# One attention and mixing kernel, with the order of its operations on all engines written anew

## The chip, the cores and the metric

The kernel runs on one core of a Trainium2 chip. Its engines work in parallel, each through its own queue in order: TensorE (PE, matrix products), VectorE (DVE), ScalarE (ACT), GpSimd (POOL) and SyncE (SP, which here only issues DMAs). An engine waits at the head of its queue until the semaphores tell that the operands are there; whatever stands behind it waits too. The metric is the device time of the core in microseconds (us), the median of several runs.

## The reference

Two blocks follow each other. The first is attention with a polynomial sketch, for 4 batches of 4 heads, 1088 tokens and 32 values a head:

```python
def phi(x):
    a = np.einsum('rd,bhsd->bhsr', S1, x)
    b = np.einsum('rd,bhsd->bhsr', S2, x)
    return np.einsum('bhsi,bhsj->bhsij', a, b).reshape(*x.shape[:-1], r * r)
q_p, k_p = (phi(q), phi(k))
kv = np.einsum('bhsf,bhsd->bhfd', k_p, v)
z = np.sum(k_p, axis=2)
num = np.einsum('bhsf,bhfd->bhsd', q_p, kv)
den = np.einsum('bhsf,bhf->bhs', q_p, z)[..., None] + 1e-06
```

with r = 8, so 64 features. Its output num / den, with the four heads side by side, is x (4 x 1088 x 128) for the second block:

```python
theta = x @ w_theta
cos_t, sin_t = (np.cos(theta), np.sin(theta))
yr = np.einsum('ts,bsd->btd', w_tok_r, x * cos_t)
yi = np.einsum('ts,bsd->btd', w_tok_i, x * sin_t)
u = x + yr + yi
return (u + np.maximum(u @ w_ch, 0.0)).astype(np.float32)
```

The two token matrices are 1088 x 1088. They, the sketch matrices and the small weights come as 64-bit floats and are turned into 32-bit ones on the chip.

## The kernel before, in words

A recording layer (`Layout`) takes down 1005 operations. Each has an engine, a function that issues one or several instructions, and the buffers that it writes and reads; its number is its place in that record. The record is the same in both kernels. Three tables then say how it is issued. `ORDER` lists all operation numbers in one sequence; each engine's queue, the DMA queues of SP, ACT and POOL among them, is the part of this sequence that belongs to it. `SLOTS` gives each of the buffers one of the numbered pieces of its memory class (22 large pieces of 1152 words, 5 for raw weights, 8 PSUM banks and so on); an operation that takes a piece over waits for the last reader of its former content. `GAPS` puts filler products (`spin`, 128 x 384, their result is never read) ahead of nine operations, 27 in all.

The stages, with names as in the code, a batch number behind them:

- **loads**: k, q and v of each batch, 576 KB each; 17 token rows `row` of 1088 KB; `loadh`, a second copy of k for three batches.
- **grid, keys, sums, rest, chain**: the keys are split into a rounded part and a remainder, and 32 x 32 products over 9 chunks give the sum of the key features exactly enough for the denominator. `sums` and `rest` use 32 columns of the TensorE array at a time. `chain` turns these sums, in turns of TensorE, DVE and ACT, into the matrix of the level products; its operations 86 to 94 are those of batch 0. The last of them, 94 (`cut`), writes what `levels` of batch 0 needs.
- **kT, kf, kv**: three transposes, an ACT copy, the feature products, a DVE outer product, then the products with v (64 columns on 32 columns of the array).
- **qscale, qT, q0, levels, den, num**: the queries are scaled and split; `levels` gives their features against the chain's result; DVE forms the denominator; `num` is the numerator.
- **theta, mix**: the phase products, sine and cosine on ACT, and the products with the token rows. `mix0` and `mix1` (batches 0 and 1) use 17 rows over 1088 tokens. Batches 2 and 3 share seven half-size products (`m1` to `m7`, `zc` and `ac` are their differences), added up by `acc`.
- **out**: the last product, and the stores.

Each weight row costs two ACT passes and two DVE passes (`weight`, lines 576 to 582) before TensorE can use it.

The operations that the text names by number are: 8 (a small ACT pass for the sketch matrix), 20 (POOL, the block form of that matrix, needed by all `kf`), 27 (DVE, a small slice of three instructions), 52 and 53 (the grid of batch 0), 55 (DVE, the rounded keys of batch 0), 57 to 65 (`sums0`), 67 to 75 (`rest0`), 78 (ACT, the squares of q of batch 0 with their sum), 79 (TensorE, the one-column product that adds this sum over the partitions), 86 (`chain0`, first products), 87 (DVE, its mask), 89 (DVE, split), 90 (second products), 94 (cut), 98 (first `kf0`), 99 (the ACT copy behind it), 101, 107 and 113 (`kv0`), 120, 126 and 132 (`kT1`), 148 to 155 (`sums1`), 158 to 168 (`rest1`), 203 and 197 (`kT2`), 205 (`kf2`), 216 (DVE, the rounded keys of batch 2), 219 to 227 (`sums2`), 229 to 237 (`rest2`), 247 (the ACT copy of `kT3`), 248 (`kf3`), 274 to 282 (`sums3`), 284 to 292 (`rest3`), 307 (first products of `chain2`), 462, 469, 476, 562, 569, 576 (`num`).

Of the kernel before, what the change touches and what calls it, by code (L numbers as in the profile page):

```python
# [31 lines left out]
RPS = 4  # L32
EARLY = (2, 60.0, 4.0)
ORDER = (
# [43 lines left out]
)  # L78
GAPS = {11: 3, 57: 3, 79: 3, 110: 1, 203: 8, 153: 1, 77: 5, 86: 2, 163: 1}
SLOTS = (  # L80
# [11 lines left out]
)  # L92
WARM = 0
LOAD_LEAD = 60.0
RAW_LEAD = 30.0
CHAINS = ((0,), (1,), (2, 3))
QPOOL = (False,) * 4
KEEP = (2, 3)
KEEP_CLS = "big"
PAIR = (2, 3)  # L100
QUADS = (2, 3)
QTURN = (3,)
XTURN = (1, 2, 3)
# [1385 lines left out]
```

## Time and profile before

| | |
|---|---|
| median of 3 runs | 215.11 us (215.11 to 215.16) |
| profiled execution | 214.93 us, span 213.2 us |
| granted TensorE clock, mean | 0.996 |
| TensorE busy | 206.8 us |
| DVE busy | 181.0 us |
| ACT busy | 113.1 us |
| POOL busy | 40.3 us |
| read from HBM | 29.84 MB |

The span is the time from the first to the last instruction of the program; the execution has 1.7 us around it. In a row of TensorE, a line such as `PE L333 MATMUL ps<-hf 128*32 128x32 bf16 x28` says: the function at line 333 issued it, the result goes to a PSUM tile, the weights are 128 rows by 32 columns of the array, 32 columns stream through, and 28 such instructions follow each other. A 32-bit product shows as two instructions. Most products are issued by one helper at line 333, so they are told apart by their tiles: `sbk,g` are feature products, `hf` the key sums, `ident` transposes, `sm,ones` sums over the partitions, `idle` fillers, `big,zs` the mixing. The time of a TensorE row includes the tail of its last product, which overlaps the next row; the difference of two starts is what the queue was held.

### The profile page before, as it was taken

The numbers are of one execution on the slowest core, as the hardware profiler recorded it, in microseconds if no ns is written. First come the engines' busy times: TensorE is split into PE (matmuls) and PEld (weight loads), VectorE is DVE, ScalarE is ACT, GpSimd is POOL, SyncE is SP. The second block draws the span as 40 slices with busy tenths as digits, with TensorE's granted clock in tenths as the row PEclk, the third lists the DMA queues.
The fourth block names the chain that finished last, engine by engine and source line by source line (L and its number), as shares of the span: only waits on it lengthen the run. The fifth ranks groups of instructions, "written<-read, shape, count | busy, mean of one in ns | idle before, by whom it ended". The sixth has DMA issues, their size and how long they took to land.

```text
span 213.2 us, 5209 instructions
## 1 busy us (share of the span) xinstructions
PE 206.8 (97%) x2092; PEld 150.0 (70%) x2092; DVE 181.0 (85%) x363; ACT 113.1 (53%) x238; POOL 40.3 (19%) x89
## 2 busy tenths in 40 slices
PE   7999999999999999999999999999999999999991
PEld 7777798968867677756686665766667768667671
DVE  1799999999999999999998999987999986583632
ACT  3899999999999699664435203686600000000000
POOL 1272730306800106600000005000400000040001
PEclk9999999999999999999999999999999999999998
DMA  6999999996996526867300005438253010070043
GB/s 217 407 416 416 377 353 422 425 347 111 358 302 205 235 114 176 346 212 276 152 0 0 3 0 86 132 113 232 51 87 65 0 31 0 3 125 1 14 75 68
DMA packets 28779, 37.05 MB, mean 174 GB/s; under 512 B 21332, under 2 KB 23812, under 8 KB 26580
## 3 DMA queue, kind: packets, MB, share of 16 engines
q1 hardware_dynamic: 23268, 31.91, 43.2%
q0 software_dynamic: 1488, 3.15, 7.1%
q10 hardware_dynamic: 4000, 1.67, 3.0%
q8 instruction: 16, 0.26, 0.5%
q14 instruction: 7, 0.06, 0.1%
HBM read 29.84 MB, written 4.00 MB: 159 GB/s over the span
## 4 chain that ended last, share of the span: by engine, by line
PE 78%; issue 10%; ACT 5%; DMA 2%; DVE 2%; POOL 1%; POOLq 0%; SPq 0%; DVEq 0%; ACTq 0%
PE ps L333 71%; PE ps L1063 2%; DMA st<-s 2%; PE ps L961 2%; ACT big L627 2%; POOL out L1246 1%; ACT g L732 1%; PE ps L362 1%; ACT big L934 1%; PE ps L729 1%; ACT big L579 1%; ACT big L577 1%; PE ps L1136 0%; DVE big L313 0%; DVE g L1250 0%
## 5 line engine op out<-in xcount | busy, mean ns | idle before, releaser
L333 PE MATMUL ps<-big,zs 128*128 128x384 f32 (+2 forms) x380 | 109.0, 435 | 0.0
L333 PEld LDWEIGHTS ps<-big,zs 128*128 128x128 f32 x380 | 67.1, 190 | 34.3 <-issue 0.5
L1287 ACT COPY g<-ps 80x256 f32<-80x256 f32 x1 | 0.4, 367 | 55.1 <-PE ps L1280 55.1
L577 ACT ACTIVATE big<-zs 128x1088 f32<-128x1088 f32 x17 | 20.8, 1226 | 6.5 <-issue 4.0
L579 ACT ACTIVATE big<-zs 128x1088 int32<-128x1088 uint32 (+1 forms) x18 | 21.4, 1191 | 3.2 <-DVE big L313 2.2
L313 DVE CUSTOM_DVE_ANT_0 big<-big,big 128x2176 uint16<-128x2176 uint16 x17 | 21.9, 1285 | 0.0
L333 PE MATMUL ps<-big,big 128*32 128x32 f32 (+2 forms) x352 | 21.7, 234 | 0.0
L313 DVE TENSOR_TENSOR big<-big,big 128x544 f32<-128x544 f32 x24 | 16.5, 715 | 2.6 <-PE ps L333 2.5
L333 PEld LDWEIGHTS ps<-big,big 128*32 128x32 f32 (+1 forms) x352 | 14.7, 124 | 4.9 <-issue 0.8
L327 POOL DMA_DIRECT2D g<-big x6 | 5.3, 1088 | 59.9 <-ACT g L1223 59.0
L1246 POOL DMA_DIRECT2D out<-g x6 | 3.8, 633 | 51.8 <-DVE g L1250 51.8
L317 DVE TENSOR_SCALAR big<-big 128x1088 int32<-128x1088 int32 x17 | 12.1, 719 | 0.0
L333 PEld LDWEIGHTS ps<-w,big 128*128 128x128 f32 (+1 forms) x76 | 9.9, 189 | 2.2 <-ACT big L1076 0.6
L362 PE MATMUL ps<-idle 128*128 128x112 bf16 (+1 forms) x67 | 10.0, 312 | 1.3 <-POOL idle L364 1.3
L313 DVE TENSOR_TENSOR g<-lv 128x768 f32<-128x768 f32 x12 | 11.0, 949 | 0.1
L320 DVE SCALAR_TENSOR_TENSOR big<-ps,even,big 128x160 f32<-128x160 f32 (+1 forms) x10 | 5.0, 495 | 7.0 <-PE ps L333 6.6
L313 DVE TENSOR_TENSOR big<-big,hf 128x1152 f32<-128x1152 f32 x8 | 10.7, 1349 | 0.0
L333 PE MATMUL ps<-w,big 128*128 128x128 f32 (+1 forms) x76 | 10.7, 278 | 0.0
L333 PE MATMUL ps<-sbk,g 128*128 128x64 f32 x72 | 10.0, 276 | 0.3 <-ACT g L732 0.3
L333 PE MATMUL ps<-mf,big 128*128 128x96 f32 (+1 forms) x72 | 10.2, 279 | 0.0
L313 DVE TENSOR_TENSOR zs<-zs,g 128x384 f32<-128x384 f32 (+2 forms) x24 | 9.9, 448 | 0.1
L333 PEld LDWEIGHTS ps<-sbk,g 128*128 128x128 f32 x72 | 9.0, 191 | 0.8 <-ACT g L732 0.6
(200 smaller groups left out, 354.8 us busy)
## 6 DMA issues: line engine op xcount, KB each, us to landing
zs<-w_tok SPq DMA_DIRECT2D x17, 1088.0 KB, 8.5
big<-k_l SPq DMA_DIRECT2D x5, 576.0 KB, 12.4
big<-v_l SPq DMA_DIRECT2D x4, 576.0 KB, 15.5
big<-q_l SPq DMA_DIRECT2D x3, 576.0 KB, 10.4
big<-hf POOLq DMA_DIRECT2D x3, 576.0 KB, 9.9
far<-zs SPq DMA_DIRECT2D x3, 576.0 KB, 3.0
zs<-far SPq DMA_DIRECT2D x12, 144.0 KB, 2.8
big<-k_l ACTq DMA_DIRECT2D x2, 576.0 KB, 4.5
```

The costliest lines, as they stand in the source:

```text
L313: eng.tensor_tensor(out=o, in0=a, in1=b, op=f)
L317: (eng or V).tensor_scalar(out=o, in0=a, scalar1=s1, scalar2=s2, op0=op0, **kw)
L320: (eng or V).scalar_tensor_tensor(out=o, in0=a, scalar=s, in1=b, op0=op0, op1=op1)
L327: op("G", 0.9, lambda: G.dma_start(dst(), src(), accum_op=ALU.add), w, r, fly=fly)
L333: T.matmul(o, lhs, rhs, start=start, stop=stop, skip_group_check=True)
L362: T.matmul(nowhere()[:, :n], idle()[:, 0:P], idle()[:, :n], start=True, stop=True, skip_group_check=True)
L577: op("A", 0.22 + n * 0.0009, lambda: A.activation(dfn(), words_of(raw(), n)[1].bitcast(F32), AF.Prelu, scale=2.0**-112, alpha=-(2.0**32)), ...
L579: op("A", 0.22 + n * 0.0009, lambda: A.activation(stp(), words_of(raw(), n)[0].bitcast(U32), AF.Copy, scale=2.0**-29), [stp], [raw])
L627: op("A", act(n) + 0.1, lambda: A.activation(flat(r()), kc(), AF.Square, accum_out=km()[:, 1:2]), [r, (km, 1)], [kx])
L961: T.transpose(tr()[:, i * P:(i + 1) * P], x()[:, g * GC + i].rearrange("p h d -> p (h d)"), ident())
L1063: T.transpose(tr()[:, i * P:(i + 1) * P], qp()[:, i * H + 2 * n:i * H + 2 * n + 2].rearrange("p h i j -> p (h i j)"), ident())
L1246: E.dma_start(out[b, s0:s0 + n, f * SQ:(f + 1) * SQ].rearrange("(c j) i -> j c i", j=SQ), ot()[f * SQ:(f + 1) * SQ, :n].rearrange("j (c i) ...
```

## The change

`ORDER` and `SLOTS` are replaced; nothing else is. The first 25 entries of `ORDER` stay, up to operation 144: the DMAs of the first ten loads and the sketch, and the first operations on them. Behind them the sequence is new on all five engines, and the buffers' pieces with it. The operations, their shapes and the nine places of the fillers (each ahead of the same operation as before) are the same. The lines of `ORDER` up to the second chain, old and new:

```diff
 ORDER = (
-    0, 1, 29, 32, 4, 2, 5, 3, 34, 30, 358, 50, 33, 102, 44, 96, 6, 108, 103, 36, 7, 51, 368, 54, 144, 8, 97, 10, 9,
-    11, 55, 109, 20, 52, 12, 57, 139, 58, 59, 60, 61, 62, 63, 126, 13, 31, 132, 56, 98, 127, 265, 14, 393, 128, 143,
-    246, 15, 145, 64, 65, 67, 68, 78, 35, 69, 16, 70, 19, 148, 149, 150, 151, 152, 269, 99, 66, 79, 247, 53, 80, 100,
-    110, 129, 17, 133, 130, 359, 25, 363, 81, 271, 83, 18, 203, 360, 361, 71, 41, 153, 104, 272, 210, 197, 353, 258,
-    45, 146, 72, 198, 73, 204, 248, 43, 259, 84, 26, 105, 362, 241, 74, 154, 325, 249, 214, 75, 82, 27, 327, 370, 106,
-    155, 270, 28, 47, 76, 250, 111, 46, 77, 147, 388, 216, 85, 328, 86, 21, 329, 326, 87, 112, 205, 88, 330, 242, 89,
-    120, 48, 243, 90, 206, 331, 121, 252, 369, 91, 332, 92, 134, 93, 101, 378, 394, 94, 122, 140, 253, 156, 107, 123,
-    141, 371, 135, 260, 169, 142, 124, 95, 441, 438, 157, 22, 136, 364, 439, 115, 444, 217, 440, 445, 174, 442, 261,
-    372, 446, 337, 443, 158, 159, 160, 161, 345, 365, 447, 266, 244, 170, 113, 448, 171, 373, 162, 354, 172, 215, 449,
-    163, 164, 165, 166, 211, 39, 191, 167, 173, 450, 114, 168, 212, 175, 245, 451, 333, 176, 192, 177, 267, 452, 338,
-    117, 37, 453, 343, 268, 334, 116, 254, 118, 454, 344, 341, 355, 178, 335, 273, 455, 193, 366, 342, 119, 199, 179,
-    456, 125, 255, 464, 346, 389, 219, 131, 457, 137, 465, 200, 467, 180, 367, 466, 458, 181, 194, 468, 49, 460, 459,
-    182, 471, 469, 461, 336, 183, 356, 462, 470, 339, 184, 472, 463, 474, 256, 138, 478, 383, 473, 475, 42, 185, 486,
-    390, 476, 480, 398, 340, 274, 374, 220, 221, 275, 276, 251, 186, 40, 277, 222, 278, 257, 544, 481, 477, 541, 488,
-    376, 494, 23, 375, 38, 489, 479, 195, 542, 496, 188, 482, 545, 497, 483, 357, 538, 484, 487, 218, 539, 546, 485,
-    543, 377, 24, 213, 187, 189, 223, 224, 225, 226, 279, 280, 498, 540, 547, 281, 548, 190, 549, 282, 284, 285, 490,
-    286, 287, 288, 289, 379, 227, 290, 291, 292, 503, 504, 505, 550, 495, 492, 491, 493, 551, 552, 553, 228, 385, 262,
-    506, 507, 263, 499, 500, 554, 229, 230, 555, 283, 293, 380, 294, 231, 556, 304, 301, 384, 232, 196, 233, 234, 235,
-    236, 502, 295, 305, 564, 395, 399, 501, 237, 565, 296, 264, 557, 413, 238, 566, 567, 568, 403, 571, 560, 561, 239,
-    558, 559, 297, 298, 569, 574, 306, 572, 386, 381, 575, 302, 382, 240, 303, 391, 562, 387, 573, 563, 576, 570, 581,
-    582, 307, 577, 308, 309, 404, 583, 584, 586, 578, 396, 310, 392, 508, 509, 311, 585, 400, 312, 595, 313, 510, 314,
+    0, 1, 29, 32, 4, 2, 5, 3, 34, 30, 358, 50, 33, 102, 44, 96, 6, 108, 103, 36, 7, 51, 368, 54, 144, 10, 35, 52, 393,
+    31, 97, 8, 9, 55, 363, 132, 126, 53, 139, 109, 11, 265, 12, 20, 143, 57, 58, 59, 60, 61, 62, 98, 127, 13, 56, 145,
+    269, 99, 14, 100, 246, 271, 15, 16, 25, 17, 63, 64, 128, 247, 78, 65, 66, 83, 79, 67, 146, 270, 68, 129, 69, 18,
+    110, 104, 360, 70, 111, 80, 84, 148, 149, 150, 112, 151, 130, 81, 45, 210, 133, 272, 46, 248, 47, 21, 359, 105,
+    249, 26, 71, 361, 106, 72, 203, 197, 147, 204, 198, 370, 250, 73, 74, 353, 82, 205, 75, 76, 41, 120, 362, 214,
+    325, 326, 77, 329, 85, 86, 87, 27, 241, 330, 88, 152, 153, 154, 155, 258, 327, 216, 328, 388, 89, 28, 331, 252,
+    253, 242, 90, 243, 121, 48, 134, 259, 206, 369, 91, 332, 92, 93, 94, 95, 122, 101, 371, 215, 135, 136, 217, 169,
+    107, 156, 113, 123, 157, 124, 394, 260, 114, 261, 373, 365, 438, 444, 266, 140, 439, 364, 440, 372, 441, 445, 446,
+    442, 158, 170, 159, 160, 443, 447, 211, 19, 23, 341, 22, 244, 343, 212, 171, 141, 115, 24, 161, 162, 191, 163,
+    164, 448, 449, 450, 245, 342, 219, 165, 166, 43, 167, 116, 142, 273, 344, 174, 220, 335, 254, 172, 192, 255, 451,
+    168, 333, 117, 175, 176, 177, 173, 336, 267, 452, 354, 334, 453, 118, 337, 345, 338, 193, 119, 199, 274, 454, 455,
+    346, 194, 178, 456, 464, 179, 125, 275, 221, 222, 131, 137, 465, 457, 180, 389, 467, 466, 460, 461, 223, 458, 181,
+    468, 256, 339, 218, 182, 459, 469, 183, 200, 138, 470, 49, 462, 471, 472, 184, 356, 340, 463, 474, 478, 185, 186,
+    479, 473, 355, 475, 486, 276, 277, 278, 480, 481, 279, 280, 224, 188, 213, 281, 488, 489, 282, 284, 251, 357, 374,
+    376, 476, 195, 541, 477, 482, 544, 545, 494, 375, 377, 283, 225, 542, 496, 484, 497, 538, 539, 483, 485, 546, 226,
+    227, 285, 286, 540, 543, 547, 287, 288, 289, 187, 268, 40, 228, 290, 257, 495, 291, 292, 366, 498, 189, 548, 490,
+    262, 549, 503, 504, 190, 229, 500, 378, 230, 380, 550, 39, 367, 551, 293, 491, 304, 294, 295, 552, 301, 302, 42,
+    196, 231, 232, 383, 233, 553, 234, 499, 379, 487, 492, 493, 554, 502, 235, 236, 263, 237, 555, 238, 239, 264, 556,
+    390, 395, 384, 37, 38, 505, 296, 501, 506, 564, 507, 565, 385, 566, 297, 567, 568, 298, 557, 398, 560, 558, 403,
+    305, 561, 571, 559, 381, 306, 569, 240, 303, 572, 573, 574, 570, 413, 307, 575, 562, 563, 382, 576, 386, 391, 308,
...
```

The rest of `ORDER` and all of `SLOTS` change in the same manner.

67 rows, old and new, of tables (ORDER, SLOTS) are left out of this document.

## The prediction

> **What bounds the kernel now.** I read the busy times first, then the engines stretch by stretch, then TensorE's own waits.
>
> ```profile
> PE 206.8 (97%) x2092; PEld 150.0 (70%) x2092; DVE 181.0 (85%) x363; ACT 113.1 (53%) x238; POOL 40.3 (19%) x89
> ```
>
> Stretches: PE, weight loads, DVE, ACT and POOL busy, granted clock, DMA share, GB/s.
>
> ```profile
> 10.00:20.00 10.00, 9.74 (x205) 7.88 (x203) 9.61 (x20) 9.88 (x26) 4.85 (x17) 1.00 1.02 418
> 20.00:30.00 10.00, 9.99 (x198) 7.94 (x198) 9.62 (x27) 9.29 (x27) 4.72 (x12) 1.00 1.02 366
> 40.00:110.00 70.00, 70.00 (x833) 49.98 (x832) 68.30 (x127) 55.96 (x103) 16.53 (x28) 1.00 0.69 232
> 110.00:205.00 95.00, 95.00 (x530) 64.75 (x529) 77.26 (x141) 22.11 (x45) 7.85 (x10) 1.00 0.27 57
> ```
>
> TensorE's waits over the whole span:
>
> ```profile
> PE ps L362 <- POOL idle L364: 1.3, 1, 1.3
> PE ps L333 <- ACT g L732: 0.3, 1, 0.3
> PE ps L333 <- DVE hf L317: 0.2, 1, 0.2
> ```
>
> TensorE is full from 10 us to the last product, and DVE is nearly full up to 110 us (68.30 of 70.00). The set of products is the same in both kernels, the 27 filler products of the gaps too. So an order can win only waits and changeover losses inside TensorE's queue; what it adds there is paid in full, since no later stretch has idle time to give back. The end (the last six products, outputs, stores) has the same operations in nearly the same order, and I cost it at nothing.
>
> **The waits that the change can take away.** TensorE's rows (start, time, operation, count):
>
> ```profile
> 6.98 0.65 PE L362 MATMUL ps<-idle 128*128 128x384 bf16 x3
> 7.70 0.27 PE L416 MATMUL ps<-ident,m 128*2 128x128 f32 x1
> 7.81 0.65 PE L362 MATMUL ps<-idle 128*128 128x384 bf16 x3
> 8.68 0.35 PE L333 MATMUL ps<-hf 128*32 128x32 bf16 x28 [0.23 <-DVE hf L317]
> ...
> 11.84 0.22 PE L333 MATMUL ps<-hf 128*32 128x32 bf16 x8
> ...
> 12.70 0.66 PE L362 MATMUL ps<-idle 128*128 128x384 bf16 x3
> 13.20 0.28 PE L333 MATMUL ps<-sm,ones 128*128 128x1 f32 x2
> ...
> 18.34 0.25 PE L333 MATMUL ps<-big,big 128*32 128x32 f32 x8
> 18.41 0.25 PE L333 MATMUL ps<-big 128*32 128x32 f32 x8
> 18.92 0.88 PE L333 MATMUL ps<-sbk,g 128*128 128x64 f32 x6 [0.26 <-ACT g L732]
> ...
> 23.58 0.25 PE L333 MATMUL ps<-sq,sm 32*32 32x16 f32 x8
> ...
> 25.59 0.83 PE L333 MATMUL ps<-sm,pbd 128*128 128x64 f32 x6
> ...
> 27.80 0.54 PE L333 MATMUL ps<-g,big 128*32 128x64 f32 x24
> ```
>
> A filler holds the queue 0.16 us (from 12.70 to 13.20 three of them pass; their 0.65 includes the last one's tail). Three from 6.98 end their issue at 7.47, the next product starts at 7.70: 0.23 lost. Three from 7.81 end at 8.30, the key sums start at 8.68: 0.38, of which 0.09 is a changeover, below. The feature product at 18.92 stands 0.44 behind the last eight strips (eight take 0.07, from 18.34 to 18.41), 0.33 of it a wait. That makes 0.23 + 0.29 + 0.33 = 0.85 us of waits. All may go: the transposes of key tile 1 (126, 132) now stand ahead of the fillers at the first two places, and the feature product 248 stands behind other work.
>
> **The waits that it adds.** I lay the new queues out by hand, each operation with its row's duration.
> First, product 79 (the query scale) needs the ACT pass 78:
>
> ```profile
> 11.74 1.15 ACT L934 ACTIVATE big<-big 128x1152 f32<-128x1152 f32 x1
> 12.80 0.19 ACT L934 ACTIVATION_READ_ACCUMULATOR big<-big 128x1 f32 x1
> 12.89 0.22 ACT L744 COPY sm<-ps 128x96 f32<-128x96 f32 x1
> ...
> 13.08 0.49 ACT L732 COPY g<-ps 128x384 f32<-128x384 f32 x1
> ```
>
> On ACT the copies 99 and 247 (0.22 and 0.49, each some 0.1 less where the next one overlaps it) move ahead of it, so it ends at about 13.5 instead of 12.98 (11.74 to 12.80 + 0.19). On TensorE most of the strip work from 11.84 to 12.70 moves behind 79, so TensorE is there at about 12.6 instead of 13.2: 0.9 us of waiting. Ahead of that, the small ACT pass 8 moves behind two copies; DVE's key rounding 55 and POOL's block 20 slide by 0.35, and the products 57 and 98 that need them wait about 0.4 together.
>
> Second, the chain of head group 0 (operations 86 to 94, TensorE, DVE and ACT in turn):
>
> ```profile
> 20.64 0.18 DVE L317 TENSOR_SCALAR psc<-ps 128x32 f32<-128x32 f32 x1
> 20.86 0.42 DVE L313 TENSOR_TENSOR psc<-ps,psc 128x32 f32<-128x32 f32 x2
> ...
> 23.22 0.87 DVE L317 TENSOR_SCALAR hf<-big,sm 128x1152 bf16<-128x1152 f32 x1
> 24.03 0.22 DVE L313 TENSOR_TENSOR sm<-ps,hm 128x64 f32<-128x64 f32 x1
> ...
> 27.83 0.16 DVE L317 TENSOR_SCALAR sm<-sm 128x4 int32<-128x4 int32 x1
> ```
>
> With the waits above, and with 205 and 120 ahead of them, the chain's first products (23.58) come at about 24.6. DVE has by then done all that stands ahead of its mask and idles some 1.3 us, from 23.8 to 25.1. Behind the mask now stand 27 (0.6, from 20.64 to 20.86 + 0.42) and 216 (0.81, from 23.22 to 24.03), so the split 89 ends at about 27.0, and TensorE, which has only short work in between, waits 0.5 us at product 90 (25.59 before, 27.1 now). The cut 94 (27.83) starts at about 29.7, with as much DVE work ahead of it as before: DVE is then 1.9 us behind. The level products come after further feature products and don't wait.
>
> Added: 0.4 + 0.9 + 0.5 = 1.8; taken away 0.85; net **+0.95 us**. Bounds: -0.85, if every new wait is covered, and +1.9, if TensorE later loses all that DVE has lost.
>
> **Changeovers.** Products on strips of the array (32 or 64 columns wide) and on the whole array:
>
> ```profile
> 33.95 0.49 PE L961 MATMUL ps<-ident,big 128*128 128x128 f32 x3
> 34.37 0.46 PE L333 MATMUL ps<-big,big 128*32 128x32 f32 x32
> 34.76 0.55 PE L961 MATMUL ps<-ident,big 128*128 128x128 f32 x3
> ...
> 39.61 0.82 PE L961 MATMUL ps<-ident,big 128*128 128x128 f32 x6
> 40.27 0.78 PE L333 MATMUL ps<-sbk,g 128*128 128x64 f32 x6
> ```
>
> Six transposes followed by whole-array work hold the queue 0.66, so three 0.33; three followed by strips hold it 0.42: 0.09 to go into strips. 32 strip products at 0.07 for eight take 0.28; they hold it 0.39: 0.11 to come out. So 0.2 for each run of strips. Counted over the queue, the old order has 34 runs and the new one 38. Up to the level products of batch 0 they are equal; behind them 14 become 18 (158 | 159, 160 | 161, 162 alone where 158 to 161 were one, 223 alone, 225 alone, 291 and 292 alone, 235 apart from 229; in exchange 113 goes in front and 307 joins 562). Four runs, all where TensorE has no idle time: **+0.8 us**; bounds 0 (they fall into waits) and 1.2.
>
> One rule speaks against this term. The Trainium skill, "TensorE: Matmul & The Clock Gate", section "Step-by-step: what each phase is for", has TensorE pull the next weights ahead of products in flight when the row groups don't conflict or the background weight buffer takes them. By it a changeover is hidden, and the sum would be the waits alone. Between whole-array products the rows agree (0.11 a transpose, without a gap); between strips and the whole array they show the 0.2.
>
> **What costs nothing.** The loads: the first ten are in place; behind them q1 goes ahead of v0, h3 and h2 come earlier, v1 and v3 later. The DMA engines are full at least to 30 us either way (share 1.02), with the same bytes.
>
> ```profile
> big<-v_l SPq DMA_DIRECT2D x4, 576.0 KB, 15.5
> ...
> 12.35 0.33 SPq L605 DMA_DIRECT2D big<-q_l x1
> ```
>
> v0 takes q1's place, issued at 12.35, and lands by 27.9 with the median; its first product stood at 27.80 and now comes near 29.5. That cover is thin, 1.6 us; if it fails, the value sums wait and the level products of batch 0 behind them. POOL's joins keep their places or come earlier. From 110 us on, DVE and ACT have room (77.26 and 22.11 of 95): a new place there costs nothing as long as each partial result is read before its bank is written again, and between product 6 and product 7 of the same bank there are now some 1.4 us of other products.
>
> **Sum.** Against the profiled execution (214.93 us, span 213.2): 214.93 + 0.95 + 0.8 = 216.7. It lies 0.18 below the median of the runs, 215.11; on that the same sum gives 216.9. I forecast **216.8 us**.
>
> **Rivals.**
> Covered (not slower): the old waits go and no new one of weight comes, because ACT gets through its early copies sooner than I laid out and 78 ends before TensorE is there. For it: these are short waits, and a few tenths on ACT decide. Against it: ACT is 9.88 of 10.00 busy there, so a pass behind 0.5 us more work does come later. 215.1 - 0.85 + 0.8 = 215.1; if the changeovers too fall where TensorE would wait, 215.1 - 0.85 = 214.3, faster. It decides where the new waits stay under 0.5 us in all (0.85 - 0.8 + 0.43). Chances 0.14 and 0.08.
> Free changeovers: only the waits count, 216.0. For it the rule above, against it the rows. 0.10.
> DVE becomes the bound: the 1.9 us it loses by 29.7 stay, since it idles only 1.7 from 40 to 110, and TensorE waits for it at the rotated level products and the second chains: 215.1 + 1.9 + 0.8 = 217.8. For it DVE's share, against it that TensorE itself comes 1 to 1.8 later, which hides most. 0.20.
> A late load: if v0 takes 3.3 us more than the median to land, it is 1.7 past its cover, 218.5. 0.06.
>
> **How the numbers follow.** The forecast itself has 0.42 (own range 216.3 to 217.3). 0.2% is 0.43 us, about what a measurement tells from no change here. Faster is 0.08, same 0.14, slower 0.42 + 0.10 + 0.20 + 0.06 = 0.78. The range 215.0 to 218.0 leaves out the 0.08 below and the late loads, and takes in the DVE bound.
>
> **What would show it.** Right: a wait of 0.5 to 1 us of the one-column product on ACT's L934 at 13 us; DVE waiting about 1 us on L333 near 25; the cut's first row near 29.7; and 0.09 and 0.11 at the two ends of each strip run, as now. Wrong: no new PE wait in the first 30 us, or a PE wait beyond 40 us, which would be a DVE or load wait; a span under 213.5 would mean that the covers hold.

## The result, and the profile after

The changed kernel takes 220.15 us in the median (219.41 to 223.46, 4 executions) against 215.13 us of the kernel before, run beside it. The ratio is 1.022, with an interval of 1.020 to 1.024: slower by 5.0 us. The forecast was 216.8 us, with 215.0 to 218.0 as its range: the direction was right, and the size a third of what came. Of the changed kernel the profiled execution took 219.41 us, with a span of 217.6 us. (The intervals given with ratios leave out executions more than 1.5% above the fastest; the medians and ranges do not.)

The first thing to see is new: before, the slices of the granted clock read 9 up to the last one, which reads 8. The page of the changed kernel, busy times and granted clock:

```profile
PE 209.4 (96%) x2092; PEld 152.4 (70%) x2092; DVE 181.5 (83%) x363; ACT 113.9 (52%) x238; POOL 44.8 (21%) x89
...
PEclk9999979999999999999999999999999999999999
```

The stretches of the changed kernel (PE, weight loads, DVE, ACT, POOL busy, granted clock, DMA share, GB/s):

```profile
10.00:20.00 10.00, 9.28 (x180) 7.53 (x178) 9.83 (x19) 9.08 (x26) 5.47 (x14) 1.00 1.02 416
20.00:30.00 10.00, 9.51 (x200) 8.00 (x202) 8.43 (x21) 8.94 (x23) 6.04 (x13) 0.97 1.03 396
30.00:40.00 10.00, 10.00 (x206) 8.92 (x198) 8.16 (x16) 7.30 (x19) 8.22 (x20) 0.86 1.02 408
40.00:110.00 70.00, 69.97 (x861) 49.89 (x856) 67.17 (x130) 58.23 (x112) 13.70 (x22) 1.00 0.67 225
...
28.00:29.00 1.00, 1.00 (x12) 1.00 (x11) 1.00 (x2) 1.00 (x2) 0.00 (x0) 1.00 1.01 320
29.00:30.00 1.00, 1.00 (x36) 0.93 (x39) 0.90 (x5) 1.00 (x4) 0.00 (x0) 0.74 1.04 331
30.00:31.00 1.00, 1.00 (x52) 1.00 (x48) 0.86 (x6) 0.81 (x5) 0.25 (x1) 0.50 1.02 333
...
32.00:33.00 1.00, 1.00 (x10) 1.00 (x10) 1.00 (x2) 0.36 (x3) 0.86 (x3) 0.55 1.02 410
```

From 10 to 20 and from 20 to 30 us TensorE falls 0.72 and 0.49 short of full, where it fell 0.26 and 0.01 short before; DVE is no fuller than before from 40 to 110 (67.17 for 68.30). TensorE is counted as busy throughout from 28 to 33 us, and still it loses time there: its clock is granted at 0.50. The trace's record of clock changes has the halving at 29.48 us and the return at 32.89, 3.41 us later.

TensorE's waits in the changed kernel:

```profile
PE ps L362 <- POOL idle L364: 1.3, 1, 1.3
PE ps L333 <- DMA g<-big: 0.7, 1, 0.7
PE ps L333 <- ACT big L934: 0.5, 1, 0.5
PE ps L333 <- DVE sm L313: 0.5, 1, 0.5
PE ps L333 <- DVE hf L317: 0.2, 1, 0.2
PE ps L333 <- POOL sq L313: 0.2, 1, 0.2
PE ps L416 <- DVE m L435: 0.2, 1, 0.2
```

Two of the forecast waits are there (on ACT's L934 and on DVE's split). Two were not forecast: 0.2 us for POOL's `sq` at 17.10 us, and a wait on the DMA `g<-big`, late in the kernel. The rows behind the three longest, on TensorE:

```profile
13.23 0.38 PE L333 MATMUL ps<-sm,ones 128*128 128x1 f32 x2 [0.52 <-ACT big L934]
...
26.97 0.83 PE L333 MATMUL ps<-sm,pbd 128*128 128x64 f32 x6 [0.49 <-DVE sm L313]
...
142.96 0.81 PE L333 MATMUL ps<-g,w 128*128 128x320 f32 x2 [0.73 <-DMA g<-big]
```

and on DVE, the idle time ahead of the mask 87, and the cut 94:

```profile
23.08 0.33 DVE L317 TENSOR_SCALAR sm<-sm 128x1 int32<-128x1 int32 x2
24.73 0.22 DVE L313 TENSOR_TENSOR sm<-ps,hm 128x64 f32<-128x64 f32 x1 [1.33 <-PE ps L333]
...
29.27 0.17 DVE L317 TENSOR_SCALAR sm<-sm 128x4 int32<-128x4 int32 x1
```

Where the time comes from is read from the starts of four operations that stand in the same order in both kernels: 90 (second products of the first chain), 442 (last level product of batch 0), 752 (first numerator product of batch 3) and 1003 (the last store). The starts in us, the last columns being the differences:

```
                     90      442      752     1003   442-752   752-1003
before             25.59    33.20   133.20   209.60   100.00    76.40
after              26.97    35.98   137.13   214.09   101.15    76.96
```

The changed kernel is 1.4 us late at 90, 2.8 us at 442, loses 1.15 more up to 752 and 0.56 behind it. So there are four places: the first 27 us, the half clock between 90 and 442, the middle, and the end. The experiments take them one by one.

One thing must be kept in mind with this table. The four operations stand in the same order, but some others have changed sides. The products 113 and 266 come ahead of 442 in the new order and behind it in the old one, where they hold the queue 0.36 and 0.14 us. So of the 2.78 us at 442, 0.50 is work done earlier, and the middle loses 0.50 more than the table says: 1.65 for the same work. In the same way 0.33 of the 1.38 at 90 are the three transposes 252 (`kT3`), which the old order has behind it. The eight products that change sides at 752 nearly cancel (2.58 us each way in the old kernel).

### The profile page after: what moved, and what is told of

Read it like the earlier page. It is cut to its first block, busy times and chain, and to the rows that moved or that the text cites. A ratio compares the mean times of both kernels' runs of the same rounds, so it can differ in the third digit from the quotient of the medians.

```text
span 217.6 us, 5203 instructions
## 1 busy us (share of the span) xinstructions
PE 209.4 (96%) x2092; PEld 152.4 (70%) x2092; DVE 181.5 (83%) x363; ACT 113.9 (52%) x238; POOL 44.8 (21%) x89
## 4 chain that ended last, share of the span: by engine, by line
PE 67%; issue 14%; DVE 9%; DMA 5%; POOL 2%; ACT 1%; POOLq 0%; SPq 0%; DVEq 0%; ACTq 0%
PE ps L333 60%; DVE big L313 3%; DMA g<-big 3%; PE ps L1063 2%; DMA st<-s 2%; PE ps L961 2%; DVE hf L317 1%; PE ps L362 1%; POOL out L1246 1%; PE ps L729 1%; POOL sx L536 1%; DVE zs L313 1%; PE ps L1136 1%; DVE sm L317 0%; DVE g L1250 0%
## 5 line engine op out<-in xcount | busy, mean ns | idle before, releaser
L333 PE MATMUL ps<-big,big 128*32 128x32 f32 (+2 forms) x352 | 23.4, 235 | 0.0
L333 PEld LDWEIGHTS ps<-big,big 128*32 128x32 f32 (+1 forms) x352 | 15.3, 125 | 6.3 <-issue 0.9
L333 PE MATMUL ps<-mf,big 128*128 128x96 f32 (+1 forms) x72 | 10.7, 282 | 0.0
L333 PE MATMUL ps<-sbk,g 128*128 128x64 f32 x72 | 10.6, 288 | 0.1
L333 PEld LDWEIGHTS ps<-sbk,g 128*128 128x128 f32 x72 | 9.6, 203 | 0.5 <-POOL sbk L313 0.2
L333 PEld LDWEIGHTS <-hf 128*32 128x32 bf16 (+1 forms) x252 | 7.9, 98 | 2.7 <-issue 0.9
```

The source lines that it names most:

```text
L333: T.matmul(o, lhs, rhs, start=start, stop=stop, skip_group_check=True)
```

## The experiments

### The clock

First, two ways to fill the thin places of the new order with fillers: eight more, or the same 27 moved.

```diff
 # e1_fill, the changed kernel
-GAPS = {11: 3, 57: 3, 79: 3, 110: 1, 203: 8, 153: 1, 77: 5, 86: 2, 163: 1}
+GAPS = {11: 3, 57: 3, 79: 3, 110: 1, 203: 8, 153: 1, 77: 5, 86: 2, 163: 1, 90: 4, 122: 2, 101: 2}
 # e1_move, the changed kernel
+GAPS = {11: 3, 57: 3, 79: 3, 110: 1, 203: 8, 153: 1, 77: 1, 86: 0, 163: 1, 90: 4, 122: 2}
```

> The changed kernel with eight fillers more: four ahead of product 90 (in its 0.5 us wait), two ahead of 122 and two ahead of 101. Theory 1 (the granted clock at half from 29.5 to 32.9 us costs some 1.5 us, in some executions more often, and comes from too little streaming in the array in the 3.4 us before): the clock stays at 1.00 from 6 to 210 us, the median falls by 1 to 1.5 us to about 218.8 and the executions agree within 0.5 us. Rival (the clock dip costs nothing, since TensorE waits for DVE there anyway): the median rises by the fillers outside the wait, 0.8 us, to about 221.

> The changed kernel with six of the seven fillers ahead of 77 and 86 put ahead of 90 (four) and 122 (two); 27 in all, as before. Theory 1 plus the chain as bound: the first products of chain 0 come 0.9 us earlier, DVE idles 1 us less ahead of its mask, and the clock stays up: about 217.5. If the clock alone counts: 218. Rival (DVE's lateness does not reach TensorE, the dip does not cost): 220, as the changed kernel.

e1_fill: 220.02 us (219.71 to 220.32). The clock is whole and the spread falls from 4 us to 0.6, but the median stays, between the two expected values. The eight fillers hold the queue 1.3 us, of which the wait at 90 hides some; at 442 the profiled execution is 0.5 ahead of the changed kernel's. It loses more than that again in the middle (102.27 us for 101.15), most of it in two pauses at 43 and 49 us for which its profile shows no operand that was waited for. What makes them is open. e1_move: 218.52 us (three executions at 218.08 to 218.60, one at 222.32), 1.6 less than the changed kernel with as many fillers. Its profiled execution has the full clock and reaches 442 at 34.46, which is 1.26 behind the old kernel instead of 2.78. The half clock thus made about 1.5 us in the profiled execution of the changed kernel. A second execution of the changed kernel (e8_again, below), which has its half clock elsewhere, says the same: from 90 to 442 it takes 7.57 us instead of 9.01, which is 1.4.

I call what halves the granted clock the gate. Does it belong to the new order? The old kernel without fillers, and without seven of them:

```diff
 # g1_nofill, the kernel before
-GAPS = {11: 3, 57: 3, 79: 3, 110: 1, 203: 8, 153: 1, 77: 5, 86: 2, 163: 1}
+GAPS = {}
 # b3_gate, the kernel before
+GAPS = {11: 3, 57: 3, 79: 3, 110: 1, 203: 8, 153: 1, 163: 1}
```

> The kernel before without any of its 27 filler products. If the clock gate closes after stretches in which TensorE streams little, whatever the order, the old order too must lose its full clock somewhere in the first 30 us, by 1.3 to 1.7 us for each stretch of 3.4 us at half speed: 217 to 220 us, differing from execution to execution. Rival, the gate has to do with the new order alone: the fillers stood mostly in waits, so the time is 213 to 215.5 and the clock is full throughout.

> The kernel before without the seven fillers ahead of 77 and 86 (between 21.9 and 23.6 us), which hold TensorE's queue 1.1 us. The stretch of 3.41 us that holds them does array work worth 0.57 of its time; without them about 0.25 to 0.3. If the gate closes where that share falls below about a third, the clock halves for the next 3.41 us, which costs 1.5 to 1.7: 215.1 less at most 1.1 plus 1.6 is 215.6 to 216.7, and executions differ by 1 to 2 us with the place of the stretches. Rival, the gate asks for waiting time of TensorE alone: its queue is as full as before, the clock stays, and the time is 214.0 to 215.1.

g1_nofill: 225.36 us (224.49 to 226.15), ratio 1.048 [1.044, 1.052]. It leaves out work that nobody reads and takes 10 us more. b3_gate: 220.28 us over ten executions, from 215.09 to 223.45, where the kernel before stayed within 214.92 to 216.42 in the 25 executions run beside it. The bill was larger than either theory's, since the clock stays at one half for several stretches in a row: in the profiled executions three in b3_gate (27.33 to 37.57 us) and ten in g1_nofill (8.26 to 42.39). The granted clock over the span in g1_nofill:

```profile
PEclk9755555799999999999999999999999999999999
```

The stretch from 27 to 37 us of b3_gate, and then of the kernel before:

```profile
27.00:37.00 10.00, 10.00 (x109) 9.52 (x110) 7.44 (x14) 5.58 (x15) 3.91 (x8) 0.52 1.03 388
```

```profile
27.00:37.00 10.00, 10.00 (x228) 9.05 (x228) 9.38 (x21) 9.40 (x22) 2.18 (x8) 1.00 1.03 391
```

TensorE is busy 10.00 of 10.00 in both, and issues 109 products instead of 228. The seven fillers had held 1.1 us of its queue; without them the time went up by 5 in the median. So the fillers are no queue time to be saved; they keep the clock.

What the gate looks at can be narrowed. In all these traces the clock changes at the ends of stretches of 3.41 us, whose place against the program (their phase) differs from one execution to the next. For each stretch I added up the products' streamed columns (a filler's 384 columns hold the queue 0.16 us; 384 columns in FP32 hold it 0.32 and count double) times the share of the array that they use. In the changed kernel the stretch ahead of the closing, 26.06 to 29.48, comes to 0.33 of full work, though TensorE waited only 0.49 us in it. Over the seventeen profiles, every stretch of 0.29 to 0.33 that began at the full clock was followed by half clock, none above 0.37 was, and those of 0.34 to 0.37 went both ways. Waiting alone does not sort them: the stretch from 142.12 us in the changed kernel, with 0.73 us of waiting, kept the full clock at 0.71 of full work, and eight of the nine that lost it waited only 0.42 to 0.52. Nor do the streamed columns without the share of the array: columns for 0.47 of the time kept the clock in the kernel before (from 23.84 us), and 0.57 to 0.69 lost it in five runs. Strip products and feature products are busy time with little array work, and with much of them the clock fell. That is how the stretches sort; what the gate itself counts isn't shown. The Trainium skill, "TensorE: Matmul & The Clock Gate", section "What's actually happening", gives a free-running window of about 3.4 us, and the traces agree (3.41, with a wandering phase); it has the clock fall after an idle window, and here it fell after one in which TensorE waited for 14% only, so the measurement decides.

How much of the median is it? The changed kernel again, unaltered, in six more executions:

> The changed kernel unaltered, in more executions. If half-clock stretches carry its spread, time and mean granted clock lie on a line: one stretch of 3.41 us takes 0.008 off the mean and should cost 1.3 to 1.7 us, and the executions with the fewest stretches lie at 218.0 to 219.4. Rival, the spread has another cause (loads, say): times differ at equal clock by more than 1 us.

220.23 us in the median (218.35 to 222.37), the same as before. Time against mean granted clock, for all ten executions:

```
clock  1.000   0.992   0.992   0.992   0.991   0.991   0.987   0.987   0.972   0.966
us    218.35  218.94  220.26  220.33  219.41  221.32  220.04  220.13  222.37  223.46
```

The ends lie as the gate has it: 218.35 with the full clock, 223.46 with the lowest. But executions of equal clock differ by up to 1.9 us, so the clock doesn't explain all of the scatter, and what does is open. Some profiles hold a pause of TensorE that they put down to nothing (`issue`): 0.4 us at 23.2 in e1_move, 0.6 at 60.1 in b4_delay. With one execution at the full clock, the gate's share of the median is about 220.2 - 218.35 = 1.9 us. The profiled 219.41, with one stretch at half clock, is only 1.06 above that one. This fits: TensorE, late by 1.4, no longer has the wait of 0.4 us for a copy of ACT that e1_move has at 40.7 and e8_again at 42.7 us.

### The join near 142 us

```diff
 # e2_join, the changed kernel; e5_join_fill does the same on e1_fill, e6_move_join on e1_move
-    ... 527, ... 533, ...
+    ... 533, 527, ...
```

(527 and 533 are POOL's DMA issues that add x to the mixing sums of `out0_1` and `out0_2`; the text calls them joins, after the helper `join`.)

> The changed kernel with POOL's adding DMA for out0_2 issued ahead of that for out0_1, as in the kernel before. Theory 2 (TensorE waits 0.7 to 0.9 us at 142 us for that DMA to land, and nothing later gives it back): the wait is gone, about 219.4 against 220.15. Rival (some other wait takes its place, as the out0_1 product comes later): no change.

> The changed kernel with the eight fillers of the filled version, which kept the clock whole, and with join 533 ahead of join 527. Without a stretch of half clock in the way the join should show what it is worth: 220.0 less 0.8 to 1.0 is 219.0 to 219.2, no wait of TensorE for a join DMA at 142 us, and a spread under 1 us. Rival, the wait at 142 turns into another one behind it: 219.8 to 220.0.

> The moved fillers of e1_move (218.5) and join 533 ahead of 527. If the terms add, 218.5 less 0.9 is 217.6. Rival, a later wait takes the join's gain: 218.2 or more.

e2_join: 222.24 us (218.72 to 222.57), more than the changed kernel, though its lowest is lower than the lowest of the four runs beside the result (219.41). e5_join_fill: 219.55 (218.17 to 222.44) against 220.02 of e1_fill. e6_move_join: 218.58 (217.90 to 221.34) against 218.52 of e1_move. By the medians nothing is shown, since the clock moves them more than the join; the profiled execution of e2_join, for one:

```profile
PEclk9975896999999999999999999999999999999999
```

The stretch behind 752 tells it apart from the clock, which is whole there in all of them. It takes 76.96 us in the changed kernel, 76.74 in e1_fill and 76.66 in e1_move; with the join mended it takes 75.97 (e2_join), 75.96 (e5_join_fill) and 75.96 (e6_move_join). So the join's place costs 1.0 us in the changed kernel and 0.7 to 0.8 in the other two. The cause stands in the rows of POOL's issues, here of the changed kernel (the time from issue to landing is the least, the median and the longest of the joins):

```profile
135.99 1.75 POOL L327 DMA_DIRECT2D g<-big  x2 [3.78 <-ACT big L1091]
...
DMA to landing us min/median/max: 3.0/3.0/6.4
```

In the kernel before, the same lines read:

```profile
131.29 0.85 POOL L327 DMA_DIRECT2D g<-big  x1 [0.94 <-ACT big L1091]
...
DMA to landing us min/median/max: 2.9/3.1/3.5
```

The second of the two issued from 135.99 on, the one of `out0_2`, takes 6.4 us instead of 3 and ends where TensorE's wait ends, at 142.96. Standing behind another join is not enough for that: in the kernel before, the join of `out0_2` was issued at 129.16, 0.64 us behind another, and took the 3.5 us that is the longest there. What is new beside it is a transfer of SyncE, which the kernel before issues at 136.34, when its joins have landed:

```profile
137.44 0.33 SPq L1108 DMA_DIRECT2D far<-zs  x1
```

By the records of the packets, the 160 KB of the second join take from 138.51 to 142.28 us, and the 576 KB of this transfer run beside them from 138.88 to 142.58. In the kernel before the packets of both joins pass from 130.01 to 132.17, with no other transfer on the way. In e1_fill, e1_move and e8_again, which have the joins in the same order, the same transfer runs beside the second join, and it takes 6.1 to 6.2 us. With 533 first, the product starts at 141.81 in e5_join_fill without a wait:

```profile
141.81 0.70 PE L333 MATMUL ps<-g,w 128*128 128x320 f32 x2
```

### Changeovers, and what a saved moment is worth

```diff
 # e3_runs, the kernel before: one filler between each two of the strip operations 158 to 166
+GAPS = {..., 159: 1, 160: 1, 161: 1, 162: 1, 164: 1, 165: 1, 166: 1}
```

> The kernel before with one filler put ahead of each of the strip products 159, 160, 161, 162, 164, 165 and 166: seven more fillers, seven more changeovers between strips and the whole array. Theory 3 (a round trip costs 0.2 us, a filler 0.16): 215.1 + 7 x 0.36 = 217.6. Rival (changeovers are hidden by weights loaded ahead): 215.1 + 7 x 0.16 = 216.3.

219.0 us (218.02 to 222.84), ratio 1.017 [1.012, 1.021]. In the trace the seven interruptions cost 2.84 us of TensorE's starts; seven fillers are 1.14 of that, so 0.24 is left for each. The lowest time, 218.02, is the 215.2 of the kernel before and 2.84; why the median lies a microsecond higher isn't shown (the execution at 219.65 had a granted clock of 0.999). The rows show one such period directly: eight strips and a filler come again after 0.46 to 0.47 us, and eight strips (0.07) and a filler (0.16) are half of that.

```profile
34.64 0.27 PE L333 MATMUL ps<-big,big 128*32 128x32 f32 x8
34.84 0.34 PE L362 MATMUL ps<-idle 128*128 128x384 bf16 x1
35.10 0.27 PE L333 MATMUL ps<-big,big 128*32 128x32 f32 x8
35.30 0.34 PE L362 MATMUL ps<-idle 128*128 128x384 bf16 x1
35.57 0.27 PE L333 MATMUL ps<-big,big 128*32 128x32 f32 x8
```

The rival of free changeovers is out. Then the reverse, the kernel before with fewer strip runs:

```diff
 # h1_merge, the kernel before (a filler moves from 163 to 113)
-    ... 101, ... 122, 140, ... 156, ... 158, ... 345, ... 266, ... 170, ... 576, ... 307 ...
+    ... 122, 140, 101, 156, ... 345, 266, 170, 158, ... 576, 307, ...
```

> The kernel before with four strip runs fewer: 122 and 140 move ahead of 101 and 156 behind it, 345, 266 and 170 move ahead of 158, and 307 moves behind 576. Changeovers cost 0.2 to 0.24 us for each run of strips that interrupts whole-array work, so four fewer should take 0.8 to 1.0 us away: 215.1 less 0.9 is 214.2. Rival, changeovers free: 215.1, no change. Rival, the moved operations wait for their DVE or ACT partners: up to 0.5 of it given back, 214.7.

215.02 us (214.79 to 215.83, ten executions) against 215.06: the same. The queue has 31 runs for 34, three fewer and not four, so 0.7 us was to be saved. In its trace, which is of the slowest of the ten, as much turns up as two waits that the kernel before does not have:

```profile
PE ps L1063 <- ACT g L764: 0.4, 1, 0.4
PE ps L333 <- ACT g L682: 0.3, 1, 0.3
```

Two runs that test the other sign, a loss of known size, in the kernel before:

```diff
 # b4_delay: six more fillers ahead of product 79
-GAPS = {... 79: 3, ...}
+GAPS = {... 79: 9, ...}
 # b2_act: the ACT copies 99 and 247 ahead of the pass 78
-    ... 78, ... 99, 66, 79, 247, ...
+    ... 99, 247, 78, ... 66, 79, ...
```

> The kernel before with six more fillers ahead of product 79, 0.98 us of TensorE's queue at 13 us, with no other engine touched. If an early loss is paid in full, as the prediction says, 215.1 plus 0.98 is 216.1. Rival, other engines' waits later take part of it up, as they took back the gain of the merged strip runs: 215.3 to 215.7.

> The kernel before with the ACT copies 99 and 247 ahead of the pass 78, nothing else. By the prediction's rows the pass ends at about 13.5 instead of 12.98 and product 79 waits 0.3 to 0.4: 215.4 to 215.5 if it is paid in full, and 215.1 if later waits take it up.

b4_delay: 216.31 us against 215.20, 1.1 for 0.98 put in (ratio 1.006 [1.003, 1.008]). b2_act: 215.74, which is 0.5 (1.003 [1.001, 1.006]); in the trace product 79 waits 0.3, and the wait for the copy ahead of 248 is 0.2 longer than in the kernel before. An early loss is paid in full; an early gain (h1_merge) is not kept.

### The parts together

```diff
 # f1_fixed, the changed kernel
-    ... 247, 78, ... 527, ... 533 ...
+    ... 78, 247, ... 533, 527 ...
+GAPS = {11: 3, 57: 3, 79: 6, 110: 1, 203: 8, 153: 1, 77: 1, 86: 0, 163: 1, 90: 4, 122: 2}
 # f2_fixed_merged: f1_fixed; e7_move_join_merge: e6_move_join; both with four strip runs fewer
-    ... 158, 170, 159, 160, ... 211, ... 161, 162, ... 225, ... 539, ... 495, 291, 292 ...
+    ... 170, 158, 159, 160, ... 161, 162, 211, ... 539, 225, ... 291, 292, 495 ...
```

> The changed kernel with the three losses mended that the traces show: join 533 ahead of join 527 on POOL (0.7 to 1.0 us), the ACT copy 247 behind the pass 78 (0.5 us of the wait at product 79), and the fillers put where TensorE now waits, three more ahead of 79, four ahead of 90, two ahead of 122, and six taken from 77 and 86 (no stretch of half clock, 1.3 us). 219.4 less 0.8 less 0.4 less 1.3 is 216.9; expected 216.9 to 217.4 and a small spread. If the order of the rest costs more than waits, changeovers and clock, it stays above 218.

> As f1_fixed, with four strip runs fewer: 170 moves ahead of 158, 161 and 162 behind 160, 225 behind 539 and 495 behind 292. By 0.2 to 0.24 us for each run 0.8 to 1.0 us less than f1_fixed, about 216.1; by the rival of free changeovers the same as f1_fixed.

> As e6_move_join with four strip runs fewer, the moves of f2. If the terms add, 217.6 less 0.85 is 216.7, and what stays above the old kernel, 1.5, is the early waits (1.0) and a rest of 0.5. Rival, covered waits of other engines come out when TensorE is earlier, as in f2: 217.2 to 217.6.

f1_fixed: 218.43 us (217.91 to 219.14). f2_fixed_merged: 217.56 (216.68 to 218.03), ratio 1.011 [1.008, 1.014]. e7_move_join_merge: 218.06 (217.08 to 221.39), 0.5 below e6_move_join. The expected 216.9, 216.1 and 216.7 were not reached. One reason is the clock: the profiled executions of f1_fixed, e6 and e7 have a half-clock stretch at about 18 us, behind the strip runs of the new order, which the moved fillers do not cover at every phase. The other is seen in the middle, from 442 to 752, where four runs fewer took off 0.54 (e6 to e7) and 0.62 (f1 to f2) instead of 0.96, the 0.24 of e3_runs four times. The wait behind it, in e6_move_join's list of waits and then at its place in e7_move_join_merge:

```profile
PE ps L916 <- ACT g L732: 0.4, 1, 0.4
```

```profile
41.92 0.33 PE L916 MATMUL ps<-ident,sm 128*128 128x128 f32 x1 [0.89 <-ACT g L732]
```

It grows from 0.4 to 0.9: half of the gain becomes waiting for a copy of ACT, as in h1_merge. It is the first half. The two runs merged ahead of this place gain 0.49 us on e6_move_join, and behind the wait nothing of it is left; the two merged behind it gain 0.46, and that is kept up to 752. From f1_fixed to f2_fixed_merged it goes the same way. No version of the new order that was run beats the kernel before.

## Why the prediction was right in direction and wrong in size

**The waits, +0.95: right in sum, not in its terms.** At 90, ahead of the half clock, the changed kernel is 1.38 us late, and 1.05 of that without the transposes 252. Of this, 0.2 is already there at 7.9 us; six profiles of the old order differ as much there (product 57 starts between 8.64 and 8.95), so that is scatter, and 0.85 is left. Of the terms, the 0.4 at products 57 and 98 did not come: 57 still waits 0.22, as before, and 98 came earlier than before. The wait at 79 is 0.52, not 0.9: of the two copies only 247 stood right ahead of the pass, which started at 11.93 for 11.74. The one at 90 is 0.49 for 0.5; DVE idles 1.33 for 1.3 ahead of the mask, and the cut starts at 29.27 for 29.7. A wait of 0.20 for POOL was not forecast. And of the 0.85 said to be taken away, most stayed: the waits on `hf` (0.2) and on `m` (0.19) stand where they stood, and only the 0.33 at 248 went. The added waits were put 0.6 too high (1.8 for 0.52 + 0.49 + 0.20) and those taken away 0.5 too high (0.85 for 0.33), so the net nearly held, by luck.

**Changeovers, +0.8: the price was right, the term for the middle too small.** The price of a run is 0.24 by e3_runs, for 0.2, and the queues do hold 34 and 38 runs (behind 442, 21 and 25 rather than 14 and 18); four runs are 0.96. But for the same work the middle lost 1.65 in the changed kernel, and 2.10 in e1_move at the full clock. 0.20 of both comes from the products that change sides at 752. In e1_move 0.41 more is the wait for ACT's copy at 40.7 us, which the prediction did not have. About 0.5 is left in both, and what it is stays open.

**What was costed at nothing is where it failed most.** Two steps:

- The sentence that an order "can win only waits and changeover losses inside TensorE's queue" left the clock out. The prediction's own rows held the granted clock, at 1.00 in every stretch, and it took that for a property of the chip where it was one of the order. It costed the fillers as queue time. The gate makes 1.4 to 1.5 us up to 442 in the profiled execution and about 1.9 of the median.
- "POOL's joins keep their places or come earlier. From 110 us on ... a new place there costs nothing": the room of DVE and ACT was looked at, but not the order of the two joins against the order of the two products that read them, nor SyncE's transfer beside them. The product of `out0_2` stood right behind 18 short products, its join behind another join and beside 576 KB of SyncE's. This makes 0.6 us against the old kernel and 1.0 against the mended order.

In numbers, for the profiled executions (219.41 and 214.93, 4.48 apart), with the same work on both sides of 442:

```
                                    forecast   came
waits, up to 442                      0.95     0.84
half clock                            0        1.44
middle, 442 to 752                    0.8      1.65
behind 752                            0        0.56
```

The first two rows divide the 2.78 - 0.50 at 442 by e8_again's 7.57 us from 90 on. At the full clock the changed kernel took 218.35 in its one execution; the clock makes the rest up to 220.2.

**The rivals.** Free changeovers: out, by e3_runs. Covered: out, the two waits came. DVE as the bound: no wait of TensorE on DVE or on a load stands beyond 40 us; TensorE's lateness there was not DVE's doing. Late load: none, v0 had landed at 27.27 when its product came at 29.31. The sign that was named, a wait of TensorE beyond 40 us, did come, but it was for a join. The lasting rule, that an early loss is paid in full, held (b4_delay). Its mirror, that a saved moment is kept, did not (h1_merge, and the first two merged runs of e7), and the prediction had leaned on it for the 0.85.

## What to carry to other kernels

Where a kernel runs close to a limit of the clock, price each stretch of a new order by the array work in it and not by TensorE's busy time, and look at the times of single executions for a spread before trusting a median; a filler may be worth several times the queue time that it takes. For each product that waits for a transfer, lay the order of the issues beside the order of the products, and the large transfers of the other queues beside both, in quiet stretches too. Before two kernels are compared between two marks, see that the same work lies between them. And count losses on a full queue in full, but gains only up to the next engine's due time: ask which copy the product will wait for when it comes half a microsecond sooner.

## What was not expected of the hardware

The clock halves for whole stretches of 3.41 us while TensorE's records show it busy nearly without a gap (waiting 0.49 of 3.41 us), once the array work of a stretch is below about a third of full; 0.34 to 0.37 went both ways. The phase of these stretches differs by execution, so one program takes from 215.09 to 223.45 us (b3_gate). Twenty-seven fillers, 4.4 us of queue time at 0.16 each, are worth 10 us.

A join of 160 KB, issued from POOL 0.56 us behind another, landed after 6.4 us where the three others nearest to it took 3.0, with 576 KB of SyncE's issued 0.89 us behind it. With no such transfer beside it, the second of two joins took 3.5 in the kernel before. The transfer was not moved by itself in any run; putting the needed join first was enough.
